# A gated linear-attention kernel with a feed-forward tail: the list of due times changed, deeper buffers for attention and output tiles, two operations on another engine

## The chip, the cores and the metric

The kernel runs on one core of a Trainium2 chip. The core has a matrix engine (TensorE, PE in the views; PEld is its weight loading), three elementwise engines (VectorE or DVE, ScalarE or ACT, GpSimd or POOL) and the SyncE queue (SP), which here only issues transfers. Each engine works through its instructions in order and waits on semaphores where it needs another engine's result. The metric is the time of one execution on the device in microseconds (us); lower is better. A profiled execution gives, beside its time, the span from the first to the last instruction of the program.

## The reference

Two stages, cut to what is computed. First a gated recurrent attention over 768 steps, for 4 batches of 8 heads with head size 40:

```
for t in range(S):
    m_new = np.maximum(f_gate[:, :, t] + m, i_gate[:, :, t])
    C = f_stab * C + i_stab * outer(v_t, k_t)
    n = f_stab * n + i_stab * k_t
    y[t] = sigmoid(o_gate[t]) * (C @ q_t) / max(|n . q_t|, 1)
```

Then a gated feed-forward part on the result laid out as 4 x 768 x 320: a causal convolution with 5 taps gives `gate`, a product with `w_val` gives `val`, and the output is `(sigmoid(gate) * val) @ w_out`. The weights and taps come as float64; everything else is float32.

## The kernel before, in words

**Tiling.** Time is cut into 6 stretches j of 128 steps (`NJ`), each into two chunks of 64 (p). A unit u is one batch of one stretch (24 units, `u = 4 j + b`), a group g is one chunk of one unit (48 groups, `g = 2 u + p`, 8 to a stretch). The recurrence becomes matrix work per group: `tr` (L270) transposes q and k on PE into `pT`, `tr_out` (L291) copies them to `qk`; `scores` (L298) multiplies them into `pss`; `args` (L319) makes the logarithm of the decay matrix in `psd` on PE from `la` and `ra`, `expo` (L332) exponentiates it on ACT into `dm`; `probs` (L337) multiplies `pss` and `dm` on DVE into `pt`; `keyw` (L347) weights the keys on POOL into `kw`; `heads` (L375) multiplies on PE into `ph` (output) and `pc` (the new state), and `state_out` (L363) copies `pc` into the value tile `vc` on ACT, where the next chunk of that batch finds it. `norm` (L395), `norm_o` (L406, tile `rs`) and `gate_o` (L412, tile `x`) divide by the denominator `den` and apply the output gate; `x_tr`, `x_copy` and `x_rest` (L418 to L442) transpose and split the result into high and low parts.

**Feed-forward.** When a stretch is done, `feed` (L805) adds for all four batches: `conv0` (POOL) and eight `conv` steps (DVE, L454) for the taps, `conv3` (PE and ACT) for the last 64 channels, `sigmoid` (ACT, L474), and for three column blocks m `val` (PE, L489), `z_mul` (DVE, L494), `z_hi` (ACT, L498) and `z_lo` (POOL, L503), then per batch `outp` (PE, L515), `outp_st` (a copy to `ob` on ACT, L520) and `out_dma` (SP, L524). The last stretch goes in two halves of two batches.

**Loads.** Per stretch SP loads q (`load_q`, tile `nat`, L174), k (`load_k`, tile `kp`, L179, per chunk and pair of batches), v (`load_v`, tile `vc`, L183), the output gate (`load_o`, inside the big tile `sg`, L186) and the spread gate factors (`spread_in`, L257 and L263). q, k, v and the output gate are 640 KB each in a stretch, in rows of 160 bytes. All are double-buffered by the parity of j, so a load for stretch j has to wait for the last reader in stretch j - 2. `sig_o` (L477) puts the output gate of stretches 0 to 2 through a sigmoid on ACT; this takes another activation table than the exponential, so a table load stands before and after it. For later stretches `sigmoid(j)` covers the output gate of stretch j + 3 as well. `load_taps` (L588, L590) and `load_weights` (L558) bring the float64 constants, and `consts2` and `weights` (L713, L720) convert and split them in many small steps on DVE, POOL and ACT (L533 to L581).

**What sets the order.** A start-up block is written out by hand for all engines (L641 to L711). All later calls go through `at(time, function)` (L745): the list is sorted by time, in units of a group, and called in that order. The times are j, u or g times their step plus an entry of `LAGS`, or a constant in the code. On SP that order is kept strictly, and within one `tr`, `scores` or `heads` call PE's order too. Otherwise the order in the list is only a priority: when the program is built, a list scheduler simulates the engines and the transfers, and gives each engine the first instruction in the list that it takes to be ready. An instruction that comes late in the list can so stand early in an engine's queue, and once it stands there, everything behind it waits. `drain` (L748) spreads the steps of `consts2` and `weights` over the list, and `tc.issue_after` keeps each of its instructions behind one given instruction of the same engine; before, these are the `keyw` and `probs` of group 1 (`last`, L743). Tiles of the pool `wk` rotate through the number of buffers that the call names; eight PSUM banks are shared out as five for `pT`, `pss`, `psd`, `px`, `pg`, `pf` and `po`, two for `ph`, one for `pc`.

## Time and profile before

| | before |
|---|---|
| median of 3 runs | 313.07 us (312.6 to 313.59) |
| profiled execution | 311.58 us |
| its span, first to last instruction | 309.6 us |
| granted TensorE clock, mean | 0.857 |
| busy: PE, DVE, ACT, POOL | 239.5, 164.3, 145.6, 145.2 us |

The profiled execution is 1.98 us longer than its span and 1.49 us shorter than the median of the runs. A row of the timeline view gives start, duration, engine, line, operation, tiles and count; in brackets stands the idle time of the engine just before it and what ended it. A row of the view by stretches gives, for each engine, busy time and number of instructions, then the granted clock, the share of time in which the 16 DMA engines were busy, and GB/s. A row of the view by lines gives the shape, the count, busy time and the mean ns of one.

### The profile page before, as it was taken

How to read it: one execution, taken by the hardware profiler on the slowest of the kernel's cores; microseconds unless marked ns; L12 is line 12 of the kernel's file. 1: busy time of each engine (PE TensorE's matmuls, PEld its weight loads, DVE VectorE, ACT ScalarE, POOL GpSimd, SP SyncE). 2: the span in 40 equal slices, each digit the busy share in tenths (PEclk: the TensorE clock that was granted, in tenths of full speed). 3: DMA queues.
4: the chain of work that ended last, by engine and by line, in shares of the span. 5: the costliest groups of instructions: out<-in, count | busy, mean ns of one | idle time of the engine just before them, and what ended most of it. 6: DMA issues, size and time to landing. Idle time of an engine off the chain costs nothing.

```text
span 309.6 us, 10479 instructions
## 1 busy us (share of the span) xinstructions
PE 239.5 (77%) x4518; PEld 188.0 (61%) x4518; DVE 164.3 (53%) x374; ACT 145.6 (47%) x286; POOL 145.2 (47%) x231
## 2 busy tenths in 40 slices
PE   2578606291629869997899994989957999999985
PEld 2456405070527657774688763867735876787984
DVE  6963004847504885527834369605286253593950
ACT  5284232451364515493455672434834445446252
POOL 5955008484504824526533345505364233684641
PEclk9895557568566959999699998999996999999999
DMA  6997999137273029911486411870000100001012
GB/s 122 164 168 117 114 139 193 29 77 124 40 110 67 4 49 126 158 24 21 74 128 152 67 23 30 104 133 25 3 0 2 66 25 3 2 30 55 26 61 85
DMA packets 109388, 22.76 MB, mean 73 GB/s; under 512 B 105320, under 2 KB 108640, under 8 KB 109344
## 3 DMA queue, kind: packets, MB, share of 16 engines
q1 hardware_dynamic: 108836, 22.01, 43.7%
q8 instruction: 35, 0.57, 0.8%
q10 hardware_dynamic: 508, 0.10, 0.3%
q14 instruction: 9, 0.07, 0.1%
HBM read 17.87 MB, written 4.23 MB: 71 GB/s over the span
## 4 chain that ended last, share of the span: by engine, by line
PE 45%; DVE 16%; DMA 11%; SPq 11%; ACT 7%; POOL 7%; issue 3%; ACTq 0%; DVEq 0%; POOLq 0%
PE ph L389 9%; PE po L515 8%; DVE sg L454 8%; PE pT L282 6%; PE pf L489 6%; DMA nat<-in_q_dram 5%; PE pg L466 4%; PE pc L391 3%; SPq L179 3%; DMA out_dram<-ob 3%; ACT sg L474 2%; PE pss L309 2%; PE psd L323 2%; PE px L423 2%; SPq L183 2%
## 5 line engine op out<-in xcount | busy, mean ns | idle before, releaser
L389 PE MATMUL ph<-vc,pt 104*64 104x41 f32 (+1 forms) x768 | 67.1, 250 | 22.1 <-DVE pt L343 15.2
L389 PEld LDWEIGHTS ph<-vc,pt 104*64 104x64 f32 (+1 forms) x768 | 58.3, 157 | 36.0 <-DVE pt L343 19.0
L354 POOL TENSOR_TENSOR kw<-kp,dm 128x320 f32<-128x320 f32 (+1 forms) x44 | 34.4, 783 | 52.8 <-PE ph L389 26.0
L391 PE MATMUL pc<-vc,kw 128*40 128x41 f32 (+1 forms) x704 | 49.2, 229 | 11.5 <-ACT vc L371 11.5
L454 DVE SCALAR_TENSOR_TENSOR sg<-xc,cwt,sg 128x512 f32<-128x512 f32 (+1 forms) x56 | 47.1, 871 | 8.8 <-POOL sg L448 8.5
L391 PEld LDWEIGHTS pc<-vc,kw 128*40 128x40 f32 (+1 forms) x704 | 42.6, 130 | 14.7 <-POOL kw L354 11.7
L282 PE MATMUL pT<-ident,nat 64*64 64x64 f32 (+1 forms) x768 | 40.1, 266 | 14.7 <-DVE sg L494 7.3
L343 DVE TENSOR_TENSOR pt<-pss,dm 128x256 f32<-128x256 f32 x96 | 36.0, 415 | 25.7 <-PE pss L313 22.5
L282 PEld LDWEIGHTS pT<-ident,nat 64*64 64x64 f32 (+1 forms) x768 | 32.9, 159 | 20.8 <-DVE sg L494 7.6
L282 PE MATMUL pT<-ident,kp 64*40 64x64 f32 (+1 forms) x768 | 35.5, 263 | 4.3 <-DMA kp<-in_k_dram 4.3
L282 PEld LDWEIGHTS pT<-ident,kp 64*64 64x64 f32 (+1 forms) x768 | 31.0, 160 | 4.8 <-DMA kp<-in_k_dram 4.8
L439 POOL TENSOR_TENSOR xl<-xc,xh 128x256 fp32r<-128x256 f32 x24 | 19.2, 800 | 27.8 <-ACT xc L432 27.5
L334 ACT ACTIVATE dm<-psd 128x512 f32<-128x512 f32 x48 | 28.5, 598 | 5.4 <-PE psd L323 2.9
L371 ACT COPY vc<-pc 40x328 f32<-40x328 f32 x44 | 18.7, 426 | 25.4 <-PE ph L389 13.9
L293 ACT COPY qk<-pT 104x512 f32<-104x512 f32 x28 | 16.0, 587 | 22.9 <-PE pT L282 22.9
L503 POOL TENSOR_TENSOR zl<-sg,zh 128x512 fp32r<-128x512 f32 (+1 forms) x14 | 16.3, 1167 | 21.5 <-ACT zh L498 21.5
L414 DVE TENSOR_TENSOR x<-ph,rs 128x320 f32<-128x320 f32 x24 | 11.8, 490 | 24.5 <-POOL rs L409 14.2
L323 PE MATMUL psd<-ra,la 120*128 120x512 bf16 x48 | 20.2, 430 | 5.4 <-ACT dm L334 2.6
L409 POOL TENSOR_TENSOR rs<-sg,den 128x320 f32<-128x320 f32 x24 | 18.0, 751 | 10.8 <-DVE den L404 10.7
L498 ACT CAST zh<-sg 128x512 fp32r<-128x512 f32 (+3 forms) x21 | 11.5, 560 | 22.8 <-DVE sg L494 22.6
L494 DVE TENSOR_TENSOR sg<-pf,sg 128x512 f32<-128x512 f32 (+3 forms) x21 | 12.6, 607 | 18.0 <-ACT sg L474 12.6
L515 PE MATMUL po<-woh,zh 128*128 128x320 f32 x72 | 19.9, 332 | 0.0
(134 smaller groups left out, 456.8 us busy)
## 6 DMA issues: line engine op xcount, KB each, us to landing
vc<-in_v_dram SPq DMA_DIRECT2D x12, 320.0 KB
sg<-in_o_gate_dram SPq DMA_DIRECT2D x6, 640.0 KB
out_dram<-ob SPq DMA_DIRECT2D x24, 160.0 KB
kp<-in_k_dram SPq DMA_DIRECT2D x22, 160.0 KB
nat<-in_q_dram SPq DMA_DIRECT2D x9, 320.0 KB
nat<-in_q_dram SPq DMA_DIRECT2D x1, 640.0 KB
rawv<-in_moe_w_val_dram SPq DMA_DIRECT2D x4, 160.0 KB
rawo<-in_moe_w_out_dram SPq DMA_DIRECT2D x4, 160.0 KB
```

The source lines that it names most:

```text
L282: nc.tensor.matmul(pT[r][i * L : i * L + m, x, h // 2], (qf, kf)[x][rows, c : c + m], ident[rows, rows], start=True, stop=True,)
L323: nc.tensor.matmul(psd, la[j % 2][:, p, b], ra[j % 2], start=True, stop=True,)
L334: nc.scalar.activation(dm, psd_[g], AF.Exp)
L343: last = nc.vector.tensor_mul(po[:, i], pss_[u][i][:, p], do[:, i])
L354: mul = (nc.vector if turn("on_dve_kw", b) else nc.gpsimd).tensor_mul(kw[0:n], kp[j % 2][0:n, p, b * H : (b + 1) * H], dmt[g][0:n, :, L - ...
L371: put(dst[n0 : n0 + D, b * H : (b + 1) * H], pct[g][n0 : n0 + D])
L389: nc.tensor.matmul(pht[u][p * L : (p + 1) * L, h], ptt[g][0:n, h], mv, start=True, stop=True)
L391: nc.tensor.matmul(pc[n0 : n0 + D, h], kwt[g][0:n, h], mv, start=True, stop=True)
L439: (nc.vector if turn("on_dve_xl", b) else nc.gpsimd).tensor_sub(xlb[j % 2][:, :, b], xb[:, :, b, 4:], xhb[j % 2].bitcast(F32)[:, :, b])
L454: nc.vector.scalar_tensor_tensor(o, xc[j % 2][:, c, b0:b1, t : t + P], cwt[:, c, t : t + 1], o, op0=ALU.mult, op1=ALU.add)
L489: nc.tensor.matmul(pf[0:n], w, x, start=(i == 0), stop=(i == len(mm) - 1))
L515: nc.tensor.matmul(pf, z, w, start=(i == 0), stop=(i == len(mm) - 1))
```

## The change

It has four parts. **Due times**: many entries of `LAGS` get other values, entries that nothing reads go, and constants of the code become entries. **Where work runs**: `on_dve_rs` goes from 0 to 2, which puts `norm_o` of batches 0 and 1 on DVE instead of POOL, and `on_dve_zl` from 0 to 1, which does so for `z_lo` of column block 0. **Buffers**: `dm` 3 to 4, `pt`, `kw`, `rs` and `x` 2 to 3, `ob` 2 to 4. **Behind what the constants are queued**: `last` becomes a dictionary that `expo`, `probs` and `keyw` write at every call, so a drained step comes behind the latest of these in the list on each of the three engines.

Sorted, the list has the loads in another order. With the names of the functions and the stretch in brackets, SP's order from the end of the start-up block is

```
before: v(1) o(1) taps w_v0 q01(2) k01(2) w_v1 w_vo q23(2) k23(2) si(2) w_o0 w_o1 v(2) o(2) q01(3) ...
after:  o(1) v(1),taps,v(1) w_v0 q01(2) k01(2) w_vo w_v1 q23(2) w_o0 v(2) w_o1 k23(2) o(2) si(2) q01(3) ...
```

(01 and 23 are pairs of batches, si is `spread_in`, w_v0 to w_o1 are the raw weights.) Later stretches repeat this: q of batches 0 and 1 comes 1.07 units earlier than before, v 0.73 earlier, k of batches 2 and 3 2.18 later, the output gate 0.34 later, the spread factors 2.80 later; in stretch 4 alone k of batches 0 and 1 comes 4.97 later.

```diff
-    "cons1": -5.183, "cons1d": 0, "cons2": 0.457, "cons2d": 2.675, "wgt": 3.44, "wgtd": 0.804, "close": 2.831,
...
+    "wgt": 4.423, "wgtd": 0.35, "close": 2.831, "den": -0.323, "dend": 0.177, "rs": 1.457, "gate": 3.86,
+    "x_tr": 4.721, "x_copy": 6.057, "x_rest": 7.056, "args": -4.274, "expo": -3.149, "scores": -2.274,
...
+    "e_ob": 9.909, "e_od": 11.211, "half": 1.641, "on_dve_state": 0, "on_dve_out": 0, "on_dve_x": 0, "on_dve_xl": 0,
+    "on_dve_rs": 2, "on_dve_kw": 0, "on_dve_zl": 1, "z@2": 13.103, "zh@2": 13.406, "zl@0": 12.032, "outp@3": 14.892,
...
+    "e_convd@1": 0, "e_ob@1": 9.928, "e_sig@3": 7.779, "cons2": 1.5, "cons2d": 0, "v1": 2.1, "o1": 0.706,
+    "taps": 2.178, "w0": 2.5, "w1": 4.989, "w2": 4.7, "w3": 7.6, "w4": 8.071, "o": -6.658, "k0": -11.55, "k1": -6.767,
+    "q0": -12.669, "q1": -9, "v": -8.126, "si": -5.697, "so1": -1.5, "so": -3.301, "tr": -4.7, "tro": -4.4,
...
     def expo(g):
-        dm = wk.tile([P, H, L], F32, name=f"dm{g}", tag="dm", bufs=3)
-        nc.scalar.activation(dm, psd_[g], AF.Exp)
+        dm = wk.tile([P, H, L], F32, name=f"dm{g}", tag="dm", bufs=4)
+        last["act"] = nc.scalar.activation(dm, psd_[g], AF.Exp).ins
...
-        pt = wk.tile([P, H, L], F32, name=f"pt{g}", tag="pt", bufs=2)
+        pt = wk.tile([P, H, L], F32, name=f"pt{g}", tag="pt", bufs=3)
...
-            last = nc.vector.tensor_mul(po[:, i], pss_[u][i][:, p], do[:, i])
+            last["dve"] = nc.vector.tensor_mul(po[:, i], pss_[u][i][:, p], do[:, i]).ins
...
-        kw = wk.tile([P, H, D], F32, name=f"kw{g}", tag="kw", bufs=2)
+        kw = wk.tile([P, H, D], F32, name=f"kw{g}", tag="kw", bufs=3)
...
+            last["pool"] = mul.ins
...
-        rs = wk.tile([P, H, D], F32, name=f"rs{u}", tag="rs", bufs=2)
+        rs = wk.tile([P, H, D], F32, name=f"rs{u}", tag="rs", bufs=3)
...
-        x = wk.tile([P, H, D], F32, name=f"x{u}", tag="x", bufs=2)
+        x = wk.tile([P, H, D], F32, name=f"x{u}", tag="x", bufs=3)
...
-        ob = wk.tile([P, DM], F32, name=f"ob{j}_{b}", tag="ob", bufs=2)
+        ob = wk.tile([P, DM], F32, name=f"ob{j}_{b}", tag="ob", bufs=4)
...
-            with tc.issue_after(last[0]), tc.issue_after(last[1]):
+            with tc.issue_after(last["pool"]), tc.issue_after(last["dve"]), tc.issue_after(last["act"]):
...
-    drain(1.5, 0.8, 1, consts2())
-    at(2.1, load_v, 1, 0)
-    at(2.2, load_v, 1, 1)
-    at(2.3, load_o, 1)
-    at(2.4, load_taps)
-    at(2.5, load_weights, "v0")
-    for t, nm in ((4.6, "v1"), (4.7, "vo"), (7.6, "o0"), (7.7, "o1")):
-        at(t, load_weights, nm)
-    drain(7.5, 0.35, 2, weights())
+    drain(T["cons2"], T["cons2d"], 1, consts2())
+    at(T["v1"], load_v, 1, 0)
+    at(T["v1"] + 0.1, load_v, 1, 1)
+    at(T["o1"], load_o, 1)
+    at(T["taps"], load_taps)
+    for i, nm in enumerate(("v0", "v1", "vo", "o0", "o1")):
+        at(T[f"w{i}"], load_weights, nm)
+    drain(T["wgt"], T["wgtd"], 2, weights())
...
-                at(t - 7.0, load_o, j)
+                at(t + lag("o", j), load_o, j)
...
-                        at(t - (11.55, 8.95)[i] + 0.1 * p, load_k, j, p, 2 * i, 2 * i + 2)
-                    at(t - 7.4 + 0.1 * p, load_v, j, p)
+                        at(t + lag(f"k{i}", j) + 0.1 * p, load_k, j, p, 2 * i, 2 * i + 2)
+                    at(t + lag("v", j) + 0.1 * p, load_v, j, p)
...
-                    at(t - (11.6, 9.0)[i], load_q, j, 2 * i, 2 * i + 2)
-                at(t - 8.5, spread_in, j, nc.sync.dma_start)
+                    at(t + lag(f"q{i}", j), load_q, j, 2 * i, 2 * i + 2)
+                at(t + lag("si", j), spread_in, j, nc.sync.dma_start)
```

More of the change, by code (lines that the diff above doesn't have):

```diff
@@ L20 @@
 LAGS = {
-    "cons1": -5.183, "cons1d": 0, "cons2": 0.457, "cons2d": 2.675, "wgt": 3.44, "wgtd": 0.804, "close": 2.831,
-    "og": -7.359, "kp": -5.611, "kpd": 1.009, "vc": -3.927, "vcd": 0.989, "nat": -14.361, "natd": 0.826,
-    "sig_o": -3.584, "max": -9.51, "hi": -8.451, "lo": -6.85, "lod": 0.308, "tr": -5.254, "den": -0.323,
-    "dend": 0.177, "rs": 1.457, "gate": 3.86, "x_tr": 4.721, "x_copy": 6.057, "x_rest": 7.056, "args": -3.401,
-    "expo": -3.399, "scores": -2.076, "probs": -1.445, "keyw": -2.703, "state": -0.531, "state_out": 0.189,
@@ L26 @@
-    "heads": -0.632, "conv0": 4.698, "conv0d": 0.9, "conv": 5.393, "convd": 0.299, "sig": 8.436, "val": 8.878,
-    "vald": 0.463, "z": 9.375, "zh": 9.181, "zl": 9.511, "outp": 13.042, "outpd": 0.257, "ob": 15.39, "od": 14.45,
-    "sig0": -0.329, "maxd": 0.014, "early": 0.441, "conv3": 8.55, "scaled": 0, "e_conv0": 5.797, "e_conv0d": 0.226,
-    "e_conv": 4.49, "e_convd": 0, "e_conv3": 3.873, "e_sig": 7.715, "e_val": 6.616, "e_vald": 0.359, "e_z": 8.556,
-    "e_zh": 8.123, "e_zl": 8.811, "e_outp": 11.131, "e_outpd": 0.989, "e_ob": 9.909, "e_od": 11.211, "half": 2.582,
@@ new lines @@
+    "x_tr": 4.721, "x_copy": 6.057, "x_rest": 7.056, "args": -4.274, "expo": -3.149, "scores": -2.274,
+    "probs": -1.445, "keyw": -2.703, "state": -0.531, "state_out": 0.189, "heads": -0.632, "conv0": 4.698,
+    "conv0d": 0.786, "conv": 5.393, "convd": 0.299, "sig": 8.436, "val": 8.878, "vald": 0.463, "z": 9.375,
+    "zh": 9.181, "zl": 9.511, "outp": 13.042, "outpd": 0.064, "ob": 15.39, "od": 14.45, "conv3": 8.55,
+    "e_conv0": 5.797, "e_conv0d": 0.226, "e_conv": 4.49, "e_convd": 0, "e_conv3": 3.873, "e_sig": 7.715,
@@ L339, in probs @@
         j, b = divmod(u, B)
-        pt = wk.tile([P, H, L], F32, name=f"pt{g}", tag="pt", bufs=2)
+        pt = wk.tile([P, H, L], F32, name=f"pt{g}", tag="pt", bufs=3)
         po, do = (t.rearrange("k (h i) l -> k i h l", i=2) for t in (pt, dmt[g]))
         for i in range(2):
-            last = nc.vector.tensor_mul(po[:, i], pss_[u][i][:, p], do[:, i])
+            last["dve"] = nc.vector.tensor_mul(po[:, i], pss_[u][i][:, p], do[:, i]).ins
         ptt[g] = pt
-        return last
     def keyw(g):
@@ L357, in keyw @@
         kwt[g] = kw
-        return mul
+        if "kw" not in last or g < 2 or T["on_dve_kw"] == 0:
+            last["pool"] = mul.ins
     pct = {}
@@ L639, in tile_mlstm_gated_ffn @@
     oh1 = sp.tile([P, H], BF16, name="oh1")
+    last = {}
     with tc.manual_schedule():
@@ L696, in tile_mlstm_gated_ffn @@
             expo(g)
-            last_pool = keyw(g)
+            keyw(g)
         for _ in range(3):
@@ L702, in tile_mlstm_gated_ffn @@
                 run(rest)
-            last_dve = probs(g)
+            probs(g)
         load_q(1, 0, B)
@@ L742, in tile_mlstm_gated_ffn @@
     work = []
-    last = (last_pool.ins, last_dve.ins)
     def at(t, fn, *a):
@@ L771, in tile_mlstm_gated_ffn @@
             if j > 1:
[L772 removed]
+                at(t + lag("o", j), load_o, j)
                 for p in range(2):
                     for i in range(2):
[L775 to L776 removed]
+                        at(t + lag(f"k{i}", j) + 0.1 * p, load_k, j, p, 2 * i, 2 * i + 2)
+                    at(t + lag("v", j) + 0.1 * p, load_v, j, p)
                 for i in range(2):
[L778 to L779 removed]
+                    at(t + lag(f"q{i}", j), load_q, j, 2 * i, 2 * i + 2)
+                at(t + lag("si", j), spread_in, j, nc.sync.dma_start)
             if j < 3:
[L781 removed]
+                at(t + T["so1" if j == 1 else "so"], sig_o, j)
     for u in range(NU):
@@ L785, in tile_mlstm_gated_ffn @@
         if u >= B:
-            at(t - 4.7, tr, u)
+            at(t + lag("tr", j), tr, u)
             for r in range(2):
-                at(t - 4.4, tr_out, u, r)
+                at(t + lag("tro", j), tr_out, u, r)
         if u > 0:
```

7 lines of the change are left out of this document (1 added, 6 removed), and 82 rows, old and new, of the table LAGS.

## The prediction

> **What bounds the kernel now.** I read the page's top first, then the busy times by stretches.
>
> ```profile
> span 309.6 us, 10479 instructions
> PE 239.5 (77%) x4518; PEld 188.0 (61%) x4518; DVE 164.3 (53%) x374; ACT 145.6 (47%) x286; POOL 145.2 (47%) x231
> PE   2578606291629869997899994989957999999985
> core 0: us, PE busy (x) PEld busy (x) DVE busy (x) ACT busy (x) POOL busy (x), PEclk, DMA share, GB/s
> 0.00:23.00 23.00, 12.09 (x371) 9.79 (x372) 17.24 (x29) 12.63 (x18) 15.55 (x36) 0.93 1.01 151
> 23.00:92.00 69.00, 33.47 (x641) 25.20 (x640) 28.06 (x75) 25.93 (x48) 29.75 (x50) 0.60 0.72 106
> 92.00:257.00 165.00, 146.08 (x3115) 113.09 (x3113) 90.84 (x210) 83.35 (x171) 73.42 (x113) 0.91 0.36 60
> 257.00:310.00 53.00, 47.81 (x400) 39.90 (x399) 28.18 (x61) 23.70 (x52) 26.48 (x34) 1.00 0.11 38
> ```
>
> The 77% of PE is an average over two kernels. From 92 us on PE is the bound: 146.1 of 165 us, then 47.8 of 53. From 23 to 92 us it works 33.5 of 69 us, at a granted clock of 0.60, and no other engine works half the time either: that part waits, for transfers and in queues. So 35.5 us lie idle early and some 24 us after that, and the change's new order of loads and constants acts on the early part. The timeline of PE gives the places.
>
> ```profile
> 47.47 0.26 PE L391 MATMUL pc<-vc,kw 128*40 128x41 f32 x1 [11.50 <-ACT vc L371]
> 60.70 0.43 PE L389 MATMUL ph<-vc,pt 128*64 128x41 f32 x2 [5.27 <-DVE pt L343]
> 73.46 0.33 PE L423 MATMUL px<-ident,x 128*128 128x128 f32 x1 [3.43 <-DVE qk L293]
> 78.97 0.44 PE L389 MATMUL ph<-vc,pt 128*64 128x41 f32 x2 [3.69 <-DVE pt L343]
> 91.20 0.33 PE L389 MATMUL ph<-vc,pt 104*64 104x41 f32 x1 [5.62 <-ACT vc L371]
> 190.52 0.37 PE L282 MATMUL pT<-ident,nat 64*64 64x64 f32 x2 [2.06 <-DVE sg L494]
> 208.05 0.31 PE L389 MATMUL ph<-vc,pt 104*64 104x41 f32 x2 [1.27 <-ACT vc L371]
> ```
>
> The first five waits are 29.5 of the 35.5 us. The engine named is not the cause; what it stood in front of is, and the timelines of ACT, DVE and SP show that.
>
> ```profile
> 43.73 1.27 ACT L477 ACTIVATE sg<-sg 128x1280 f32<-128x1280 f32 x1 [9.53 <-DMA sg<-in_o_gate_dram]
> 88.13 1.28 ACT L477 ACT_TABLE_LOAD   x1 [5.52 <-DMA sg<-in_o_gate_dram]
> 44.67 0.17 DVE L533 TENSOR_SCALAR ca_c<-rawc 128x15 int32<-128x15 int32 x1 [12.12 <-DMA rawc<-in_moe_conv_w_dram]
> 70.51 0.88 DVE L533 TENSOR_SCALAR ca_o<-rawo 128x320 int32<-128x320 int32 x1 [3.96 <-DMA rawo<-in_moe_w_out_dram]
> 32.52 2.01 SPq L183 DMA_DIRECT2D vc<-in_v_dram  x2
> 34.57 2.19 SPq L186 DMA_DIRECT2D sg<-in_o_gate_dram  x1
> 54.38 10.45 SPq L179 DMA_DIRECT2D kp<-in_k_dram  x2
> 66.84 2.44 SPq L558 DMA_DIRECT2D rawo<-in_moe_w_out_dram  x4
> 82.49 0.41 SPq L186 DMA_DIRECT2D sg<-in_o_gate_dram  x1
> ```
>
> ACT stands 9.53 us in front of `sig_o(1)` until the output gate of stretch 1 has landed, and the state copy that PE needs is queued behind it. In the same time DVE stands 12.12 us in front of the taps. At 70.5 us DVE waits for raw `w_out`, whose load SP could issue only at 66.84, because the k load ahead of it took 10.45 us, nearly all of it waiting for buffers.
>
> **The change part by part.** The sum is made against the profiled execution, 311.58 us, which is 1.49 below the median.
>
> *Output gate ahead of v.* `load_o(1)` passes both `load_v(1)` and the taps pass one of them. SP issues it 2.0 us sooner (row 32.52), and by the bytes it lands up to 0.655 MB / 120 GB/s = 5.5 us sooner, with the rate of this row:
>
> ```profile
> 30.00:45.00 15.00, 5.97 (x88) 3.91 (x85) 1.47 (x5) 3.58 (x4) 0.74 (x1) 0.50 1.07 120
> ```
>
> The DMA share of 1.07 says that the engines were full, so bytes count more than issue times. But a load that the scheduler takes to land sooner can bring `sig_o(1)` further forward on ACT: only six of the 48 exponentials ran before it, though by the list `expo(6)` (2.6) comes long before it (6.5). One group less done before the wait costs about what one does in the later stretch, 165 us over 32 groups or 5.2 us; then the gain is gone. Taps no longer hold up `pt`, since their steps now stand behind `probs(5)`: the last of them before 4.423, each being due at g - 0.99. Next late is then v(1), needed only from group 8. I take 3.0 us, between issue and bytes; bounds a gain of 5.5 and a loss of 2.
>
> *Raw w_out ahead of the k load.* `w_o0` leaves SP behind q23(2), no longer behind k23(2) and si(2). The 3.96 us of DVE and PE's 3.43 go: 3.4 us; bounds 0 (if DVE finds another wait) and 3.4. What is moved back for it, k23(2), is first read by the transposes at 15.3 in the list, six units after its new place 9.2, some 31 us.
>
> *Constants queued behind attention.* 36 conversion steps, two per draw, now begin at 4.423 and end near 10.4 instead of 7.5 to 13.5, but each behind the newest `probs`, `expo` and `keyw` in the list and not behind group 1's. The waits at 60.70 and 78.97, 9.0 us, are `pt` standing behind such steps. The steps stay and still wait for each other across DVE, POOL and ACT, so most of this is only spread out. I take 1.0; bounds a gain of 9.0 and a loss of 2 if they now meet the first `conv` of stretch 0.
>
> *Second output gate.* `load_o(2)` waits for the last `norm_o` of stretch 0 before and after, and `sig_o(2)` stands 3.4 units behind it, formerly 3.5. I take 0; bounds 0 and a gain of 5.6 (row 91.20).
>
> *Spread factors and output gates later.* si(3) now comes at 18.30 in the list and `args(24)` at 18.86: 0.55 units, 2.9 us at 5.2 per unit, against 5.0 units before. Its three issues and their landing may fill that; PE would stand once. I take 0, bounds 0 and a loss of 2. o(3) has cover: SP issued it at 120.43 and ACT used it from 133.33; 0.6 units are 3.1 us of these 12.9, and such a load landed 5.6 us after its issue (82.49 to 88.13).
>
> ```profile
> 120.43 0.41 SPq L186 DMA_DIRECT2D sg<-in_o_gate_dram  x1
> 133.33 1.28 ACT L474 ACT_TABLE_LOAD   x1
> ```
>
> *Buffers.* ACT waits for an output transfer to free `ob`, the longest time here, with `vc` queued behind it:
>
> ```profile
> 207.12 0.43 ACT L520 COPY ob<-po 128x320 f32<-128x320 f32 x1 [4.36 <-DMA out_dram<-ob]
> DVE x L414 <- POOL rs L409: 14.2, 16, 2.0
> ```
>
> With four buffers, one for each batch, that wait and PE's 1.27 us at 208.05 go: 1.3 us, lower bound 0. The deeper `dm`, `pt`, `kw` let ACT, DVE and POOL run ahead; I give nothing for it, since five PSUM banks still limit how far.
>
> *Two operations onto DVE.* Rows by shape:
>
> ```profile
> L409 POOL TENSOR_TENSOR rs<-sg,den 128x320 f32<-128x320 f32 x24 | 18.0, 751 | 10.8 <-DVE den L404 10.7
> L503 POOL TENSOR_TENSOR zl<-sg,zh 128x512 fp32r<-128x512 f32 x10 | 13.4, 1338 | 14.5 <-ACT zh L498 14.5
> L414 DVE TENSOR_TENSOR x<-ph,rs 128x320 f32<-128x320 f32 x24 | 11.8, 490 | 24.5 <-POOL rs L409 14.2 <-PE px L423 10.0
> L494 DVE TENSOR_TENSOR sg<-pf,sg 128x512 f32<-128x512 f32 x10 | 6.9, 688 | 14.8 <-ACT sg L474 10.0 <-PE px L423 3.1 <-PE pf L489 1.7
> L454 DVE SCALAR_TENSOR_TENSOR sg<-xc,cwt,sg 128x512 f32<-128x512 f32 x40 | 38.4, 976 | 8.1 <-POOL sg L448 7.7
> ```
>
> DVE gets 12 `rs` and, with the two half-width ones as one, 6 `zl`: at the rates of `x` and `z` 12 x 0.49 + 6 x 0.69 = 10.0 us; at the rate of `conv`, which like them reads two SBUF tiles, 0.976 for 512 and by width 0.61 for 320, 12 x 0.61 + 6 x 0.976 = 13.2. It saves half of the 14.2 us in which DVE waited for `rs`, 7.1, and `conv0`, which waits for this `zl`, comes 1.34 - 0.98 to 0.69 = 0.4 to 0.65 us sooner in six places, 2 to 4 us. Net between a gain of 1 and, with nothing of the `conv0` part on the path, a loss of 6. I take 0, near the lower price.
>
> *The last half's due times* (`half`) move priorities where PE is busy 47.8 of 53 us: 0, within 1 either way.
>
> Sum: 3.0 + 3.4 + 1.0 + 1.3 = 8.7. 311.58 - 8.7 = 302.9 profiled, 304.4 as a median: **304 us**. The bounds of the unknown costs put this case at 299 to 310.
>
> **The rivals.**
>
> *The early part runs at the speed of its transfers.* From 23 to 92 us 69 x 106 = 7.3 MB moved; at the 151 GB/s of the first 23 us that takes 48 us, so 21 us could go: 290.6, as a median 292. For it: five of the waits are queue order, not work. Against: the transfers wait for buffers that attention frees, and a wait that goes has another close behind it, as taps behind the output gate.
>
> *DVE becomes the bound in the changes of stretch: slower.* PE's waits there end with DVE (row 190.52), and this change puts 10 to 13.2 us more on DVE. Its place is the run of `conv` steps:
>
> ```profile
> 103.86 6.42 DVE L454 SCALAR_TENSOR_TENSOR sg<-xc,cwt,sg 128x512 f32<-128x512 f32 x7
> 184.04 3.72 DVE L454 SCALAR_TENSOR_TENSOR sg<-xc,cwt,sg 128x512 f32<-128x512 f32 x3
> ```
>
> A step took 0.92 us in the first row and 1.24 in the second, where POOL worked beside it. If the moved work is paid in full at the upper price with only the 7.1 us back (6.1), if `sig_o(1)` moves forward as far as its load (0), and constants meet the `conv` of stretch 0 (2), then 311.58 + 8.1 - 3.4 for `w_o0` = 316.3, as a median 318. It decides from the point where DVE's wait for `rs` shrinks by less than its busy time grows. [...]
>
> *Stalls only move.* What is freed early is waited for at `load_o(2)` and later: within 0.3% (1 us, about what a measurement of this kernel can tell from no change) of 313.
>
> **How the numbers follow.** Forecast 0.52, transfers' speed 0.15, no change 0.10, slower 0.23. Faster is the first two, 0.67. The range goes from 294, which leaves out the far end of the second case, to 317, which leaves out the far half of the slower one.
>
> **What would show it.** `sig_o(1)` waiting clearly under 9.5 us and PE's 11.5 us gap shorter; no wait for rawo; no `ob` wait for output transfers; DVE's wait for `rs` about halved; PE idle from 92 us on unchanged. Wrong would be the forecast if the first 92 us are not shorter by about 7 us, or if PE's busy share after them falls.

## The result, and the profile after

The changed kernel takes 284.32 us, the median of four runs (281.83 to 285.97), where the kernel before took 313.33 beside it. The ratio is 0.9075, with an interval of 0.8982 to 0.9168. The sign was right and the size was not: the profiled execution took 281.83 us where 302.9 was forecast, a gain of 29.75 us instead of 8.7, and 284 lies below the whole range.

The top of the page, after:

```profile
span 280.1 us, 10460 instructions
PE 235.4 (84%) x4518; PEld 184.9 (66%) x4518; DVE 181.2 (65%) x393; ACT 146.2 (52%) x286; POOL 129.2 (46%) x212
PE   2585939760959999997899996999968999999995
```

PE does the same 4518 matmuls in 235.4 us instead of 239.5, so 44.7 us of the span are idle on PE instead of 70.1. Most of the gain, 25.4 of 29.5 us, is idle time of PE. The view by stretches, with the first three bounds as before (the last one reaches 0.9 us past the end of the span):

```profile
0.00:23.00 23.00, 11.70 (x334) 9.43 (x334) 17.15 (x29) 13.05 (x18) 12.77 (x33) 0.93 1.02 152
23.00:92.00 69.00, 49.35 (x1041) 37.25 (x1042) 45.48 (x105) 34.67 (x68) 40.86 (x64) 0.67 0.75 114
92.00:257.00 165.00, 154.70 (x3003) 119.66 (x3004) 104.56 (x234) 89.78 (x182) 67.38 (x106) 0.95 0.37 61
257.00:281.00 24.00, 19.68 (x142) 18.55 (x140) 13.99 (x27) 8.71 (x20) 8.21 (x11) 0.96 0.16 56
```

From 23 to 92 us PE now works 49.4 of 69 us, not 33.5. From 92 us to the end of the span it idles 10.3 + 3.4 = 13.7 us, not 18.9 + 4.8 = 23.7. The places that the prediction named, first in the timeline of PE, then of ACT and of SP (start, duration, and in brackets the idle time before):

```profile
39.25 0.33 PE L370 MATMUL ph<-vc,pt 104*64 104x41 f32 x1 [4.40 <-ACT vc L352]
...
69.60 0.33 PE L370 MATMUL ph<-vc,pt 104*64 104x41 f32 x1 [6.62 <-ACT vc L352]
```

ACT, in the same view:

```profile
37.48 1.27 ACT L458 ACTIVATE sg<-sg 128x1280 f32<-128x1280 f32 x1 [6.35 <-DMA sg<-in_o_gate_dram]
...
65.18 0.49 ACT L527 ACTIVATE cm_vo<-rawvo 128x320 f32<-128x320 f32 x1 [2.77 <-POOL ce_vo L523]
...
71.48 1.27 ACT L458 ACTIVATE sg<-sg 128x1280 f32<-128x1280 f32 x1
```

SP:

```profile
31.13 0.40 SPq L167 DMA_DIRECT2D sg<-in_o_gate_dram  x1
31.57 3.91 SPq L164 DMA_DIRECT2D vc<-in_v_dram  x1
...
50.74 3.33 SPq L539 DMA_DIRECT2D rawo<-in_moe_w_out_dram  x2
...
61.94 1.29 SPq L167 DMA_DIRECT2D sg<-in_o_gate_dram  x1
```

Lines of the body stand 19 lower than in the kernel before. The output gate of stretch 1 has landed by 37.48 us instead of 43.73, and PE's gap behind it is 4.40 instead of 11.50 us. That of stretch 2 is issued at 61.94 instead of 82.49, and ACT no longer waits for it. The waits, as engine, tile and line, what it waited for, total, times and longest:

```profile
PE ph L370 <- ACT vc L352: 13.0, 4, 6.6
...
DVE x L395 <- POOL rs L390: 5.8, 9, 1.0
```

There is no wait for rawo any more and none of `ob` for an output transfer, and DVE's wait for `rs` fell from 14.2 to 5.8 us. The largest group left on PE is four waits for state copies, 13.0 us. The longest, 6.6 us, lies at 63 to 70 us, where ACT works and waits in the conversions of `w_val` and `w_out`.

**A way to split the gain.** From here on I cut each profile where the `heads` of group 16 begin, when two stretches of attention are done, and take for each part the idle time of PE, its length less PE's busy time. Before, and then after:

```profile
0.00:119.30 119.30, 68.71 (x1554) 53.21 (x1554) 62.92 (x146) 50.39 (x92) 58.94 (x105) 0.70 0.68 101
119.30:309.60 190.30, 170.75 (x2967) 134.76 (x2965) 101.40 (x229) 95.23 (x195) 86.25 (x127) 0.96 0.31 56
```

The changed kernel, in the same view:

```profile
0.00:104.40 104.40, 73.35 (x1616) 56.26 (x1616) 69.03 (x153) 51.95 (x96) 59.21 (x105) 0.71 0.76 115
104.40:280.10 175.70, 162.09 (x2907) 128.63 (x2904) 112.15 (x240) 94.27 (x190) 70.02 (x107) 0.99 0.35 61
```

Early idle fell from 50.6 to 31.1 us, by 19.5, and late idle from 19.6 to 13.6, by 5.9. PE's busy time fell by 4.0 in all, since the same work ran at a higher granted clock late, 0.99 instead of 0.96. These three make the 29.5 us by which the span is shorter. In length the early part is 14.9 us shorter and the late one 14.6. The split is not exact: the changed kernel has 62 matmuls more in its early part. And idle time is not time by itself: kernels 5 and 10 below have nearly the same early idle time, 46.9 and 46.5 us, but begin group 16 at 121.9 and 117.8 us, with PE 75.1 and 71.3 us busy at a granted clock of 0.66 and 0.71. So the table below also has the time at which the `heads` of group 16 begin.

The ratios below compare only executions within 1.5% of the fastest of the same kernel, the medians are over all, and as kernels 2, 3, 6, 8 and 14 were profiled in a slower execution, only idle time and waits are read from their profiles and, with reserve, when group 16 begins.

### The profile page after: what moved, and what is told of

It is laid out like the page before. It is cut to its first block, busy times and chain, and to the rows that moved or that the text cites. A ratio compares the mean times of both kernels' runs of the same rounds, so it can differ in the third digit from the quotient of the medians.

```text
span 280.1 us, 10460 instructions
## 1 busy us (share of the span) xinstructions
PE 235.4 (84%) x4518; PEld 184.9 (66%) x4518; DVE 181.2 (65%) x393; ACT 146.2 (52%) x286; POOL 129.2 (46%) x212
## 4 chain that ended last, share of the span: by engine, by line
PE 50%; DVE 18%; ACT 6%; issue 5%; POOL 5%; DMA 4%; SPq 2%; ACTq 0%; POOLq 0%; DVEq 0%
PE po L496 10%; PE ph L370 10%; DVE sg L435 9%; PE pf L470 7%; PE pg L447 5%; PE pT L263 5%; PE pss L290 3%; PE psd L304 3%; PE pc L372 2%; DMA sg<-in_o_gate_dram 2%; PE px L404 2%; PE pss L294 2%; DVE pt L324 2%; DMA rawv<-in_moe_w_val_dram 2%; SPq L539 1%
## 5 line engine op out<-in xcount | busy, mean ns | idle before, releaser
L370 PE MATMUL ph<-vc,pt 128*64 128x41 f32 (+1 forms) x768 | 64.0, 248 | 13.3 <-ACT vc L352 13.0
L370 PEld LDWEIGHTS ph<-vc,pt 128*64 128x64 f32 (+1 forms) x768 | 56.7, 156 | 26.3 <-ACT vc L352 14.5
L435 DVE SCALAR_TENSOR_TENSOR sg<-xc,cwt,sg 128x512 f32<-128x512 f32 (+1 forms) x56 | 49.2, 906 | 1.9 <-POOL sg L429 1.5
L263 PE MATMUL pT<-ident,nat 64*64 64x64 f32 (+1 forms) x768 | 33.9, 256 | 9.4 <-DMA nat<-in_q_dram 4.8
L263 PEld LDWEIGHTS pT<-ident,nat 64*64 64x64 f32 (+1 forms) x768 | 28.2, 152 | 14.2 <-issue 7.1
L263 PE MATMUL pT<-ident,kp 64*64 64x64 f32 (+1 forms) x768 | 31.9, 254 | 3.8 <-DMA kp<-in_k_dram 3.8
L263 PEld LDWEIGHTS pT<-ident,kp 64*64 64x64 f32 (+1 forms) x768 | 27.8, 154 | 4.9 <-DMA kp<-in_k_dram 4.3
L290 PE MATMUL pss<-qk,qk 40*64 40x64 f32 x768 | 21.4, 244 | 5.9 <-ACT dm L315 3.8
L290 PEld LDWEIGHTS pss<-qk,qk 40*64 40x64 f32 x768 | 17.2, 151 | 10.8 <-issue 4.1
L274 ACT COPY qk<-pT 104x512 f32<-104x512 f32 x28 | 16.0, 585 | 15.7 <-PE pT L263 11.4
L496 PE MATMUL po<-wol,zh 128*128 128x320 f32 x72 | 18.3, 309 | 0.0
```

Source lines behind the costliest of these rows:

```text
L263: nc.tensor.matmul(pT[r][i * L : i * L + m, x, h // 2], (qf, kf)[x][rows, c : c + m], ident[rows, rows], start=True, stop=True,)
L290: nc.tensor.matmul(o, k[p][r, h], q[p][r, h], start=True, stop=True)
L370: nc.tensor.matmul(pht[u][p * L : (p + 1) * L, h], ptt[g][0:n, h], mv, start=True, stop=True)
L435: nc.vector.scalar_tensor_tensor(o, xc[j % 2][:, c, b0:b1, t : t + P], cwt[:, c, t : t + 1], o, op0=ALU.mult, op1=ALU.add)
L496: nc.tensor.matmul(pf, z, w, start=(i == 0), stop=(i == len(mm) - 1))
```

## The experiments

The theory after the result was: the loads and the constants make the early gain, each much more than was forecast, and the late gain is due times and buffers working together. The rivals were: the buffers alone do it; the parts add up, each worth the same in either kernel; the move to DVE is what costs or gains. Kernels 1 to 4, 7, 8, 12 and 18 are the changed kernel with something undone or, in 18, taken further, the others the kernel before with something added. In the table, ratio is to the kernel before, early and late are PE's idle time in us as above, at 16 is when the `heads` of group 16 begin, busy is all of PE's busy time. Where the text compares kernels in per cent, it takes differences of these ratios, so per cent of the time before.

| | kernel | median us | ratio, interval | early | late | at 16 | busy |
|---|---|---|---|---|---|---|---|
| | before | 313.33 | 1 | 50.6 | 19.6 | 119.3 | 239.5 |
| | after | 284.32 | 0.9075 (0.8982 to 0.9168) | 31.1 | 13.6 | 104.4 | 235.4 |
| 1 | after, old loads | 288.09 | 0.9163 (0.9094 to 0.9232) | 38.6 | 12.4 | 105.8 | 234.4 |
| 2 | after, constants behind group 1 | 292.90 | 0.9317 (0.9250 to 0.9384) | 37.2 | 15.0 | 110.2 | |
| 3 | after, old buffers | 312.43 | 0.9947 (0.9902 to 0.9993) | 34.7 | 23.8 | 104.8 | |
| 4 | after, nothing moved to DVE | 288.85 | 0.9195 (0.9128 to 0.9262) | 31.8 | 12.2 | 106.3 | 243.5 |
| 5 | before + buffers | 311.85 | 0.9940 (0.9894 to 0.9986) | 46.9 | 15.4 | 121.9 | 247.5 |
| 6 | before + constants | 312.56 | no interval; runs 304.28 to 314.46 | 43.9 | 19.7 | 115.3 | |
| 7 | after, `pt` 2 | 291.67 | 0.9345 (0.9267 to 0.9422) | 30.5 | 15.3 | 103.0 | 243.4 |
| 8 | after, `ob` 2 | 296.88 | 0.9330 (0.9237 to 0.9423) | 31.7 | 18.5 | 104.1 | |
| 9 | before + due times of the computing steps | 317.51 | 1.0143 (1.0005 to 1.0280) | 47.0 | 18.9 | 118.0 | 245.7 |
| 10 | 9 + buffers | 301.89 | 0.9632 (0.9537 to 0.9728) | 46.5 | 11.9 | 117.8 | 238.8 |
| 11 | before + all but those due times | 292.50 | 0.9346 (0.9274 to 0.9418) | 30.7 | 15.6 | 103.1 | 245.4 |
| 12 | after, old `args`, `expo`, `scores` times | 295.77 | 0.9448 (0.9375 to 0.9520) | 30.5 | 17.5 | 105.0 | 245.3 |
| 13 | before + loads | 318.59 | 1.0179 (1.0085 to 1.0274) | 38.7 | 23.7 | 113.3 | 254.8 |
| 14 | 13 + constants | 313.96 | 0.9923 (0.9879 to 0.9967) | 34.9 | 25.4 | 106.1 | |
| 15 | 9 + `ob` 4 | 307.15 | 0.9867 (0.9820 to 0.9915) | 50.2 | 13.0 | 119.6 | 241.4 |
| 16 | 9 + `pt` 3 | 312.32 | 0.9984 (0.9927 to 1.0042) | 49.0 | 17.0 | 120.7 | 242.1 |
| 17 | 14 + `ob` 4 | 302.39 | 0.9661 (0.9594 to 0.9728) | 34.9 | 17.0 | 108.7 | 250.0 |
| 18 | after, all `rs` on DVE | 286.41 | 0.9177 (0.9138 to 0.9216) | 33.0 | 13.3 | 104.1 | 237.9 |

**1. The old order of loads in the changed kernel.**

```diff
-    at(T["v1"], load_v, 1, 0)
-    at(T["v1"] + 0.1, load_v, 1, 1)
-    at(T["o1"], load_o, 1)
+    at(2.1, load_v, 1, 0)
+    at(2.2, load_v, 1, 1)
+    at(2.3, load_o, 1)
...
-                at(t + lag("o", j), load_o, j)
+                at(t - 7.0, load_o, j)
...
-                at(t + lag("si", j), spread_in, j, nc.sync.dma_start)
+                at(t - 8.5, spread_in, j, nc.sync.dma_start)
```

> The changed kernel with the due times of all loads (q, k, v, output gate, spread factors, taps, raw weights) as before, the rest of the change kept. Theory 1 (SP's order made the early gain): most of the 21 us by group 8 are lost, 300 to 307 us, and ACT again waits 9 us for the second output gate. Theory 2 (the constants' place behind attention made it): 285 to 290 us. Theory 3 (deeper buffers): 285 to 290 us.

Early idle rises by 7.6 us, and PE's gap behind the output gate is 8.77 us instead of 4.40. The time rises less: 288.09 us is what was expected if the loads had not made the early gain, the intervals of the two ratios overlap, and group 16 comes only 1.4 us later. So with the rest of the change in place the loads are worth 7.6 us of PE's idle time in the early part; a gain in time from them is not shown here.

**2. The constants behind group 1 only, and not on ACT.**

```diff
+    last0 = dict(last)
...
-            with tc.issue_after(last["pool"]), tc.issue_after(last["dve"]), tc.issue_after(last["act"]):
+            with tc.issue_after(last0["pool"]), tc.issue_after(last0["dve"]):
```

> The changed kernel with the drained steps of the constants queued behind group 1 only, as before, and not at all on ACT. Theory 1: 284 to 288 us. Theory 2: the conversions run ahead of attention again, 295 to 305 us. Theory 3: 284 to 288 us.

Early idle rises by 6.1 us, and the ratio by 2.4%, clear of the change's interval; 292.90 us lies between the two ranges expected. How it acts is seen on ACT, where a conversion (`cm`) can stand at the head of the queue while POOL still works on what it needs. The groups of ACT, before (busy, mean ns, then the idle time ahead of them):

```profile
L546 ACT ACTIVATE cm_o<-rawo 128x320 f32<-128x320 f32 x2 | 1.0, 495 | 8.4 <-POOL ce_o L542 8.4
L546 ACT ACTIVATE cm_v<-rawv 128x320 f32<-128x320 f32 x2 | 1.0, 494 | 7.2 <-POOL ce_v L542 7.2
```

and after:

```profile
L527 ACT ACTIVATE cm_o<-rawo 128x320 f32<-128x320 f32 x2 | 1.0, 506 | 1.6 <-POOL ce_o L523 1.6
L527 ACT ACTIVATE cm_v<-rawv 128x320 f32<-128x320 f32 x2 | 1.0, 496 | 2.7 <-POOL ce_v L523 2.7
```

and in kernel 2:

```profile
L527 ACT ACTIVATE cm_v<-rawv 128x320 f32<-128x320 f32 x2 | 1.0, 498 | 11.0 <-POOL ce_v L523 11.0
L527 ACT ACTIVATE cm_o<-rawo 128x320 f32<-128x320 f32 x2 | 1.0, 494 | 6.8 <-POOL ce_o L523 6.8
```

Four copies of half a microsecond had held ACT for 15.6 us, with state copies and exponentials queued behind them. In the change it is 4.3 us, with the old `issue_after` 17.8 again, and in the kernel before with the constants alone (kernel 6) 5.1. A fifth copy, `cm_vo`, adds 1.7 us before, 2.8 after and 1.6 in kernel 2.

**3 and 5. All buffer counts: taken out of the change, and added to the kernel before.**

```diff
-        pt = wk.tile([P, H, L], F32, name=f"pt{g}", tag="pt", bufs=3)
+        pt = wk.tile([P, H, L], F32, name=f"pt{g}", tag="pt", bufs=2)
...
-        ob = wk.tile([P, DM], F32, name=f"ob{j}_{b}", tag="ob", bufs=4)
+        ob = wk.tile([P, DM], F32, name=f"ob{j}_{b}", tag="ob", bufs=2)
```

(`dm`, `kw`, `rs` and `x` likewise; 5 is the same edit the other way round in the kernel before.)

> The changed kernel with the buffer counts of before (dm 3, pt, kw, rs, x and ob 2). Theory 1: only the wait for ob returns, 285 to 287 us. Theory 2: the same. Theory 3 (buffers made what is gained from 92 us on, 8 us, and part of the early gain): 293 us or more, with PE's waits at each change of stretch back.

> The kernel before with the deeper buffers alone. If buffers by themselves make the gain (taking them away from the changed kernel cost 28 us): 285 to 293 us. If they only pay together with the new due times, which ask for work further ahead: 303 to 313 us. The prediction's own account (1.3 us, for ob): 311 to 313 us.

The same six numbers give 0.6% in the old order, and without them nearly the whole change is lost. The rival that buffers alone do it falls, and so does, for the time, the one that parts add up. The buffers take 3.7 us off the early idle time in either kernel (34.7 to 31.1 and 50.6 to 46.9), but no time: in the kernel before, group 16 begins at 121.9 us with them and at 119.3 without.

**4 and 18. The move to DVE: undone, and taken further.**

```diff
-    "on_dve_rs": 2, "on_dve_kw": 0, "on_dve_zl": 1, "z@2": 13.103, "zh@2": 13.406, "zl@0": 12.032, "outp@3": 14.892,
+    "on_dve_rs": 0, "on_dve_kw": 0, "on_dve_zl": 0, "z@2": 13.103, "zh@2": 13.406, "zl@0": 12.032, "outp@3": 14.892,
```

(in 18, `"on_dve_rs": 4` and `zl` as in the change.)

> The changed kernel with norm_o and z_lo all on POOL. If the move cost nothing on balance, as the prediction had it: 283 to 286 us. If it is part of the later gain, each change of stretch is longer by 1 us or more: 288 us or more. If it cost time: under 282 us.

> The changed kernel with norm_o of all four batches on DVE. Moving two of four gave 4.5 us with z_lo. If the gain is DVE's saved wait for POOL (15.7 us without the move, 5.8 with it): 280 to 283 us. If DVE is full by now at the changes of stretch: 285 to 289 us.

Without the move PE's idle time is 44.0 us instead of 44.7, with all four `rs` on DVE 46.2. Both run longer than the change (by 1.2% and 1.0%), but the intervals overlap, and the time that lies between them is PE's busy time at a lower granted clock, 243.5 and 237.9 us against 235.4, with 0.94 and 0.96 late instead of 0.99. So no gain or loss of the move itself is shown, though by the ranges on record kernel 4 would make the move part of the later gain. What the operations cost on DVE is seen by shapes, after:

```profile
L435 DVE SCALAR_TENSOR_TENSOR sg<-xc,cwt,sg 128x512 f32<-128x512 f32 x40 | 40.3, 1020 | 1.9 <-POOL sg L429 1.5
...
L390 DVE TENSOR_TENSOR rs<-sg,den 128x320 f32<-128x320 f32 x12 | 7.7, 641 | 0.4
L484 DVE TENSOR_TENSOR zl<-sg,zh 128x512 fp32r<-128x512 f32 x5 | 3.5, 691 | 2.0 <-ACT zh L479 2.0
L484 DVE TENSOR_TENSOR zl<-sg,zh 128x256 fp32r<-128x256 f32 x2 | 0.9, 472 | 0.2
```

and in kernel 4, with nothing moved:

```profile
L435 DVE SCALAR_TENSOR_TENSOR sg<-xc,cwt,sg 128x512 f32<-128x512 f32 x40 | 40.5, 1029 | 5.8 <-POOL sg L429 5.4
```

A `conv` step takes 1.02 us with the move and 1.03 without it; both are means of steps between 0.74 and 1.9 us, which the part on the rivals takes apart.

**6, 13 and 14. In the kernel before: the constants alone, the loads alone, both.** For the loads, the edit of 1 the other way round (the due times of the change for all loads); for the constants, with `last` written as in the change,

```diff
...
-            with tc.issue_after(last[0]), tc.issue_after(last[1]):
+            with tc.issue_after(last["pool"]), tc.issue_after(last["dve"]), tc.issue_after(last["act"]):
...
-    drain(1.5, 0.8, 1, consts2())
+    drain(1.5, 0, 1, consts2())
...
-    drain(7.5, 0.35, 2, weights())
+    drain(4.423, 0.35, 2, weights())
```

> The kernel before with the constants' steps alone changed: queued behind the newest keyw, probs and expo in the list, and drawn from 4.423 (consts2 all at 1.5). If this makes the early gain (taking the queueing away from the changed kernel cost 8.6 us): 300 to 306 us, with heads of group 8 near 62 us, not 79. If the early gain needs the loads too: 308 to 313 us. The prediction's account: 312 us.

> The kernel before with the new order of loads alone. The prediction's account, 3.0 us for the output gate and 3.4 us for raw w_out: 305 to 308 us. If loads and the constants' place only gain together: 311 to 315 us, the time before group 8 shortened by less than 5 us.

> The kernel before with the new order of loads and the constants' steps queued behind attention; due times of the other steps, engines and buffers as before. If these two together are the whole early gain: heads of group 8 by 58 to 60 us, heads of group 16 by 103 to 106 us, 294 to 300 us. If the buffers or the move to DVE have a part in it: heads of group 16 at 110 us or later, over 302 us.

Early idle falls by 6.7 us with the constants, by 11.9 with the loads and by 15.7 with both, out of the 19.5 of the whole change. The buffers' 3.7 would make up the rest, but the due times of the computing steps alone take off 3.6 as well (kernel 9), so what the last 3.8 are is not shown. In time, group 16 begins 4.0, 6.0 and 13.2 us earlier, out of 14.9; in kernel 17, with the same early part and the same idle time in it at a granted clock of 0.69 instead of 0.86, it is 10.6. So the two together bring their sum or more, and most of the early gain. What a kernel keeps of that to its end is another matter. Three executions of kernel 6 took 311.07 to 314.46 us and one 304.28, so its time isn't settled. Kernel 14 was expected at 294 to 300 us if it reached group 16 by 103 to 106; it came there at 106.1 and took 313.96. And the loads alone, expected at 305 to 308 or 311 to 315 us, make the kernel 1.8% slower. Kernel 13, cut at group 16:

```profile
0.00:113.30 113.30, 74.62 (x1553) 57.33 (x1553) 63.63 (x147) 51.01 (x94) 58.84 (x106) 0.68 0.71 103
113.30:317.20 203.90, 180.21 (x2967) 141.75 (x2965) 100.87 (x227) 95.02 (x194) 85.79 (x126) 0.91 0.31 54
```

The late part has grown from 190.3 to 203.9 us, 4.1 us of it idle time and 9.5 us busy time at a granted clock of 0.91 instead of 0.96. Its ACT timeline at the end of a stretch, and SP's:

```profile
151.99 0.43 ACT L521 COPY ob<-po 128x320 f32<-128x320 f32 x1
155.29 0.43 ACT L521 COPY ob<-po 128x320 f32<-128x320 f32 x1 [0.85 <-PE po L516]
163.28 0.43 ACT L521 COPY ob<-po 128x320 f32<-128x320 f32 x1 [6.59 <-DMA out_dram<-ob]
```

SP's queue over the same time:

```profile
154.35 5.65 SPq L180 DMA_DIRECT2D kp<-in_k_dram  x2
160.10 0.60 SPq L525 DMA_DIRECT2D out_dram<-ob  x1
```

And PE's:

```profile
163.75 0.38 PE L324 MATMUL psd<-ra,la 120*128 120x512 bf16 x1 [3.06 <-ACT ob L521]
```

A load of k stands at the head of SP's queue for 5.65 us, waiting for its buffer. By its place in the list it is the one for batches 0 and 1 of stretch 4, which the change moves back by 4.97 units, to just ahead of the output transfers. (In that stretch q of batches 0 and 1 comes 0.59 units later too, not 1.07 earlier.) The first of these, whose `ob` was filled by 152.4, can go only at 160.10. With two `ob` tiles ACT's third copy waits 6.59 us for it, all that ACT does for attention waits too, and PE stands 3.06 us.

**17. Loads, constants, and four `ob`.** Kernel 14 with one more line:

```diff
-        ob = wk.tile([P, DM], F32, name=f"ob{j}_{b}", tag="ob", bufs=2)
+        ob = wk.tile([P, DM], F32, name=f"ob{j}_{b}", tag="ob", bufs=4)
```

> The kernel before with the new order of loads, the constants queued behind attention, and four ob buffers; all else as before. In the version without the buffers the early gain of 13 us by group 16 was given back in the stretches from group 24 to 40 (50.1 and 52.2 us, before 41.6 and 48.0), where the third ob copy on ACT waits up to 6.2 us for output transfers that SP now issues behind late loads. If that wait is what gives it back: these stretches at 42 to 45 us, 294 to 301 us in all. If the new order of loads needs the other buffers or due times: 306 us or more.

302.39 us lies between the two ranges, 1.4 above the upper end of the first; of the two stretches from group 24 to 40, expected at 42 to 45 us, the first takes 44.3 and the second 48.9. The ratio falls from 0.9923 to 0.9661, some 8 us, and the waits for output transfers are gone. Cut at group 16:

```profile
0.00:108.70 108.70, 73.76 (x1554) 55.79 (x1554) 65.65 (x147) 50.63 (x94) 60.81 (x106) 0.69 0.74 108
108.70:301.90 193.20, 176.20 (x2966) 139.37 (x2965) 100.75 (x227) 95.03 (x194) 85.69 (x126) 0.93 0.33 57
```

Late idle falls from 25.4 to 17.0 us. So the wait for `ob` is what took most of the early gain back, and a buffer that was priced at 1.3 us is worth six times that once the loads have moved. Not all is explained: the part is still 2.9 us longer than before the change, at a clock of 0.93 instead of 0.96.

**7 and 8. In the changed kernel, one buffer count at a time:** `pt` back to 2, and `ob` back to 2 (lines as in 3).

> The changed kernel with two pt buffers, everything else kept. If the third pt is what lets probs stand ahead of the conv steps at each change of stretch: 295 to 310 us, most of what all buffers together cost. If the loss comes from ACT standing in front of ob, or from x and kw: 284 to 288 us.

> The changed kernel with two ob buffers, everything else kept. If ACT's wait for output transfers (9.7 us in two waits in the version with all buffers as before) is passed on to PE: 290 to 296 us. The prediction's account: 1.3 us, 285 to 287 us. If pt made it all: 284 to 286 us.

By the ratio they cost 2.7 and 2.6%. 291.67 us with two `pt` lies between the ranges expected; with two `ob`, the executions that the ratio compares took 291.22 and 292.19 us, as expected if the wait is passed on to PE. With two `ob` the wait is there again, though due times and all else are new:

```profile
ACT ob L501 <- DMA out_dram<-ob: 9.9, 2, 6.6
```

and late idle rises by 4.9 us. With two `pt` idle time rises by 1.1 us only; the rest is busy time, 8.0 us more, at a granted clock of 0.95 instead of 0.99 late.

**9, 10, 15 and 16. The due times of the computing steps in the kernel before: alone, with all buffers, with `ob`, with `pt`.** In 9 the table of the change is used, the loads and constants keep their old places, and nothing goes to DVE:

```diff
-    "dend": 0.177, "rs": 1.457, "gate": 3.86, "x_tr": 4.721, "x_copy": 6.057, "x_rest": 7.056, "args": -3.401,
-    "expo": -3.399, "scores": -2.076, "probs": -1.445, "keyw": -2.703, "state": -0.531, "state_out": 0.189,
+    "x_tr": 4.721, "x_copy": 6.057, "x_rest": 7.056, "args": -4.274, "expo": -3.149, "scores": -2.274,
+    "probs": -1.445, "keyw": -2.703, "state": -0.531, "state_out": 0.189, "heads": -0.632, "conv0": 4.698,
...
```

The others add buffer lines of 3 the other way round.

> The kernel before with the new due times of the computing steps alone (args, expo, scores, the feed-forward's, the last half); loads, constants, engines and buffers as before. Theory 4 (the later gain needs due times and buffers together): no faster than before, 311 to 320 us. If due times alone carry the later gain: 298 to 306 us.

> The same with the deeper buffers too; loads, constants and engines as before. Theory 4: the stretches from group 16 on take about 40 us as in the changed kernel, 298 to 303 us, and the early part is as before (heads of group 8 at 79 us). If the later gain needs the move to DVE or the early part to be ahead: 308 us or more.

> The kernel before with the new due times of the computing steps and four ob buffers, the other buffers as before. Due times alone measured 317.5 us, with all buffers 301.9. If ob is the buffer that due times need: 302 to 306 us. If pt, x and kw are: 312 to 317 us.

> The kernel before with the new due times of the computing steps and three pt buffers, the other buffers as before. If pt is the buffer that due times need: 302 to 306 us. If ob is: 310 to 317 us. If they need both: between, 306 to 312 us for each.

Alone the due times lose 1.4%, by an interval that just leaves out no change; with the buffers they win 3.7%, where the buffers alone won 0.6%. Of the two buffers tried singly `ob` wins more (from 1.0143 to 0.9867) and `pt` less (to 0.9984), and neither reaches the whole set. Late idle goes 19.6, 18.9 (due times), 15.4 (buffers), 11.9 (both).

**11 and 12. The due times of the computing steps missing:** the kernel before with loads, constants, buffers and the move to DVE, but the old due times for the rest; and the changed kernel with three of the entries as before (and their entries for single stretches):

```diff
-    "tr@5": -4.587, "k0@4": -6.582, "w2d@4": 0.132,
+    "tr@5": -4.587, "k0@4": -6.582, "w2d@4": 0.132, "args": -3.401, "expo": -3.399, "scores": -2.076, "args@3": -3.45, ...
```

> The kernel before with everything of the change but the computing steps' due times: loads, constants, engines and buffers as in the changed kernel. Theory 4: the early gain of 15 to 20 us stays, the later one is missing, 295 to 300 us. If due times do nothing: 284 to 287 us. If each part only works in the finished order: over 305 us.

> The changed kernel with args, expo and scores due as before (args 0.87 later, expo 0.25 and scores 0.20 back), the rest of the change kept. If these three are the due times that let deeper buffers pay: 295 us or more. If the feed-forward's and the last half's due times matter: 284 to 288 us.

Both are slower than the change, by 2.7 and 3.7% and clear of its interval, with 1.6 and 3.3 us more of idle time and some 10 us more of busy time, at a clock of 0.94 to 0.95 late. Three old entries in the new table (295.09 to 296.42 us) are worse than the whole old table (291.94 to 293.36, below the 295 to 300 expected). In steps, late idle goes from 19.6 before to 25.4 with loads and constants (14), 17.0 with four `ob` (17), 15.6 with the other buffers and the move to DVE (11), and 13.6 with the due times.

Part of what the due times are worth is thus idle time, and the larger part is clock: late, PE is busy for 172.9 us at 0.94 in kernel 11 and 170.8 at 0.95 in kernel 12, and for 162.1 at 0.99 in the change. None of these kernels runs faster than the change.

## Why the prediction was right in its sign and wrong in its size

In the terms of its sum: for the early part it took 3.0 + 3.4 + 1.0 = 7.4 us, and idle time fell by 19.5; for the late part 1.3, and it fell by 5.9; for PE's speed nothing, and its busy time fell by 4.0.

- **Output gate ahead of v, 3.0.** Mis-sized. The gate was there 6.25 us sooner, more than the bound of 5.5. The feared move of `sig_o(1)` was there too: ACT came to it at 31.1 instead of 34.2 us, with two state copies done ahead of it and not three, so its wait fell by 3.2 only, and yet PE's gap shrank by 7.1. All of the new loads, priced at 6.4 with the next term, took 11.9 us of early idle time in kernel 13.
- **Raw w_out ahead of the k load, 3.4.** The wait is gone, but the load is not what ends it: kernel 13, with the loads alone, still has it with 3.9 us (last row below), and kernels 1 and 6, with the old loads and the constants placed anew, do not have it.
- **Constants queued behind attention, 1.0.** This is the step that failed early. The prediction saw `pt` behind conversions on DVE and took that wait to be only spread out. The runs showed conversions at the head of ACT, 15.6 us of waiting in four copies, of which the new `issue_after` leaves 4.3; the term measured 6.1 (kernel 2) and 6.7 us (kernel 6) of PE's idle time, and 3.8 on top of the loads (13 to 14). It is not all gone: PE's 6.6 us at 63 to 70 us are a state copy behind conversions.
- **Second output gate, 0.** The far bound came: ACT's 5.52 us of waiting are gone, and no wait of PE over 1 us stands behind it any more.
- **Later spread factors, 0.** Right: PE's one wait for them is 0.4 us, and was 0.6.
- **Buffers, 1.3.** This is the step that failed late. The wait for `ob` was read in the old order and its price taken over. In the new order the loads put output transfers behind waiting k loads, and the same two tiles cost some 8 us (kernels 14 and 17, 8). The others, for which nothing was given since "five PSUM banks still limit how far", take 2.4% more on top of `ob` with the new due times (15 and 10); PE's idle time falls by 4.8 us with them.
- **Two operations onto DVE, 0.** Right as far as idle time shows. They took 7.7 + 3.5 + 0.9 = 12.1 us, within 10.0 to 13.2, and the wait for `rs` fell by 8.4.
- **The last half, 0 within 1.** Too narrow: from the `heads` of group 40 to the end it was 63.1 us and is 59.2. The due times alone give 61.2 (kernel 9), with buffers 59.5 (kernel 10).
- **"PE idle from 92 us on unchanged"** was wrong: 13.7 instead of 23.7 us.
- **The bounds.** The upper bounds that the prediction names, 5.5 + 3.4 + 9.0 + 5.6 + 1.3 + 1 + 1, add up to 26.8 us, 284.8 profiled. It put this case at 299 to 310 without a sum for that. The measured gain is 2.9 us beyond even the sum of the bounds.

```profile
ACT ob L521 <- DMA out_dram<-ob: 13.8, 4, 6.6
...
DVE ca_o L534 <- DMA rawo<-in_moe_w_out_dram: 3.9, 1, 3.9
```

(Waits of kernel 13.)

**The rivals.** The early part at the speed of its transfers, 21 us, was given 0.15, and it came as far as group 8: its `heads` begin at 57.8 instead of 79.0 us, and up to there the transfers are busy for 0.97 of the time at 149 GB/s, not 0.83 at 122. These are the rows up to there, before and after:

```profile
0.00:79.00 79.00, 38.97 (x862) 29.61 (x862) 41.52 (x93) 32.20 (x54) 41.36 (x78) 0.69 0.83 122
```

The changed kernel:

```profile
0.00:57.80 57.80, 39.31 (x922) 30.01 (x922) 33.84 (x77) 30.14 (x50) 30.87 (x68) 0.76 0.97 149
```

But 57.8 x 149 = 8.6 MB have moved by then and not 79.0 x 122 = 9.6 MB, so the new order also asks for less ahead of group 8. At group 16 14.9 us are left of the 21.2, because the next stretch takes 46.6 instead of 40.3 us. And the other half of the gain lies behind group 16, of which this rival said nothing; that its 292 us is the nearest of the four is in part luck. The range, which began at 294, left it out.

The slower rival, DVE as the bound, did not come: a `conv` step takes longer than before the change (1.020 against 0.976 us), but just as long without the move (1.029). What POOL has to do with the price of a moved operation is seen in the single instructions. These are two `rs` and the `kw` on POOL beside the second:

```profile
43.03 0.49 DVE L390 TENSOR_TENSOR rs<-sg,den 128x320 f32<-128x320 f32 x1
...
108.94 0.69 DVE L390 TENSOR_TENSOR rs<-sg,den 128x320 f32<-128x320 f32 x1
```

```profile
108.55 0.74 POOL L334 TENSOR_TENSOR kw<-kp,dm 128x320 f32<-128x320 f32 x1 [1.81 <-PE ph L370]
```

Three of the 12 `rs` on DVE began with POOL idle or at the end of a short copy and took 0.49 us, as long as `x`, which has one input in PSUM. The other nine began while POOL was in `kw` or `ce_o`, took 0.55 to 1.14 us, and each ended 0.34 to 0.35 us after POOL's instruction. Of the five `zl` of full width none began inside such an instruction, but for the last 0.1 us of one, and they took 0.69 us, as `z` does (0.688). `conv` varies in the same way: with POOL idle a step of full width takes 0.74 us before and after the change, beside a busy POOL 1.12 and 1.15 on average and up to 1.9. So in these traces `rs` has two prices, 0.49 us beside an idle POOL and one that follows from when POOL's instruction ends, and the upper price of the prediction, taken from the mean of `conv`, was near for `rs` (0.641 against 0.61) and wrong for `zl` (0.691 against 0.976) by where they fell. The prediction's two `conv` rows don't differ as it read them: POOL worked beside both, and each holds steps of 0.74 us and longer ones.

## What to carry to other kernels

Price a buffer, and any wait, in the order that the change will make and not in the one that the trace shows: ask which transfer will stand at the head of its queue, and what is queued behind it. When several parts of a schedule change together, one alone can lose where all win, so test by undoing parts as well as by doing them. And compare PE's idle and busy time separately before crediting a difference to an edit, since the clock moves the second: here the 2967 matmuls of the late part took 170.75 us at 0.96 in the kernel before and 180.21 at 0.91 in kernel 13.
